# Softmax in PSUM, one subtraction for the rests of the turned probabilities, and global jobs in other slots

## The chip, the cores and the metric

The kernel runs on one core of a Trainium2 chip. The metric is the device time of one execution in microseconds (us). Five instruction streams of the core matter: TensorE (PE, matrix products, with its weight loads as PEld), VectorE (DVE), ScalarE (ACT), GpSimd (POOL) and SyncE (SP), which here only issues DMA transfers. SBUF is the working memory, PSUM the memory into which TensorE writes.

## The reference

Local and global attention over 8 batches and 8 heads, followed by a two-layer network. Per head there are 512 local and 32 global positions of 64 values each. A local query sees the 32 global keys and the local keys at most 32 positions away; a global query sees all 544 keys.

```python
s_g = scale * np.matmul(q_g, k_all.transpose(0, 1, 3, 2))
out_g = np.matmul(sm(s_g), v_all)
mask = np.abs(pos[:, None] - pos[None, :]) <= window
s_ll = np.where(mask, s_ll, -1000000000.0)
s_l = np.concatenate([s_lg, s_ll], axis=-1)
out_l = np.matmul(sm(s_l), np.concatenate([v_g, v_l], axis=2))
# x: the outputs of all heads side by side, 4352 tokens x 512
h = np.maximum(x @ w_in, 0.0)      # 512 -> 2048
return (h * h @ w_out)             # 2048 -> 512
```

`sm` is the softmax with 1e-9 added to the sum.

## The kernel before

**Slots.** The whole kernel is one loop over slots t = 0 to 145 (line 614). In slot t the local attention of head-half t (128 of them: 8 batches, 2 halves of 256 queries, 8 heads; 8 head-halves make one block of 256 tokens) is taken through scores and softmax, and finished in slot t + 1. Step m = t - 9 of the network runs in the same slot: 8 steps for each of 17 blocks, the last of which holds the global tokens. One step is 256 of the 2048 hidden columns: `gemm1` (tile h, two halves j), `act1` (relu and square, into pt), `act2` (gh) and, a slot later, `gemm2` (tile o, accumulated over the eight steps and brought out by `evac`).

**Split values.** From slot 16 on (`plain` is false) every product is made of rounded operands (float32r, "hi") and the rests that rounding left ("lo"): a b is hi hi + hi lo + lo hi. So every operand is rounded by a ScalarE copy (qk, v, ph, gh, x_h, gvh, pth) and gets its rest by a VectorE subtraction (second half of qk, v, the parts of ph/ml/pl, gl, x_l, gvl, ptl). The names in brackets are the tiles under which the profile shows them. Before slot 16 plain float32 products are used.

**One local head-half** from slot 16 on: `scores` (line 155; four products into one PSUM bank, tile s, with the small global score product gs beside it), `softmax1` (VectorE: add the mask, negate, and take the minimum, into the SBUF tile prob, twice 224 columns), `softmax2` (ScalarE: exponential in place in prob, with row sums into st), `softmax3` (VectorE: add 1e-9, reciprocal, two multiplications in place), `turn` (GpSimd copies the 16-bit halves of prob apart into planes in three copies, and a DMA transposes them into turned). In slot t + 1 `join` (GpSimd) puts the halves together in joined; `parts` (ScalarE) rounds them to ph; `parts_rest` (lines 243 to 248) makes three rests: into a quarter of ph, into ml (128 columns) and into pl (256 columns); `av` multiplies with v into the PSUM tile xa (nine products), and `x_evac` in slot t + 2 copies it to x_h and x_l.

**Global jobs.** A group of four heads of a batch is done in two pairs. Once its scores are collected in sg, a table (lines 694 to 709) lays its steps on slots and on places within a slot: `g_soft`, `g_exp`, `g_norm`, `g_turn`, `g_join` as for the local heads, `g_parts` (pth, ptl), `g_split_v` (gvh, gvl), `g_av` (13 products into tile gxo, which uses xa's bank, and a scaled copy to gxs) and `g_x` (four VectorE transposes of 32 x 32 into xg). There are 16 groups, so 32 pairs.

**Order.** Each engine's instructions keep the order in which the program text issues them (class `InOrder`, line 43) once the slot reaches 17; an instruction that waits holds up all behind it on its engine. Plain `nc.sync` transfers (gv, qr, weights, outputs) are placed by the scheduler. The pool p1 has one buffer for each tag, p2 two. raw (a head's input) has two buffers: the load of head t + 2 waits until head t's raw was last read, by the rest of v. The scores' bank s, the bank of xa and pt are single.

In slot t TensorE runs s, h (j = 0), h (j = 1), gs, o (j = 0), gxo if there is one, o (j = 1), xa. The loop's core around the change, before:

```python
if run: gemm1(m, 0)
split_v(t); softmax2(t); parts(t - 1)
softmax3(t); turn(t); load_head(t + 2)
# jobs at places 4 and 3, gemm1(m, 1), g_scores
split_qk(t + 1); act1(m)
parts_rest(t - 1); split_qk_rest(t + 1)
# gemm2(m - 1, 0), jobs at place 0, gemm2(m - 1, 1)
av(t - 1); act2(m)
```

## Time and profile before

| what | value |
|---|---|
| median of 3 runs | 1070.45 us (1070.18 to 1073.39) |
| profiled execution, own time | 1071.19 us |
| its span, first to last instruction | 1069.1 us |
| mean granted TensorE clock | 0.994 |
| busy TensorE / VectorE / ScalarE / GpSimd | 1029.5 / 867.7 / 721.5 / 385.0 us |
| slots 22 to 127 (first scores to first scores) | 798.55 us |

In rows of the profile the first name is the written tile and the names behind the arrow are read; nearly all lines carry L53, the helper that keeps the order, so groups are told apart by their tiles. A group's row ends with its busy time, the mean of one instruction in ns, and the idle time of its engine just before it with what ended that. In the timeline and in the chain of waits the first number is the start and the second the length, in us. In a table of stretches each engine's busy time is followed by its number of instructions, in the order PE, PEld, DVE, ACT, POOL, then the granted clock, the DMA share and GB/s. In a table of waits the numbers are the total in us, how often, and the longest.

### The profile page before, as it was taken

What the parts mean: (1) busy time and instruction counts of PE and PEld (TensorE: products, weight loads), DVE (VectorE), ACT (ScalarE), POOL (GpSimd) and SP (SyncE); (2) the same over time, 40 slices, a digit from 0 to 9 for tenths busy, and PEclk for the clock granted to TensorE, in tenths of its full rate; (3) what the DMA queues carried; (4) which work ended last, traced back from release to release, by engine and by line L of the source; (5) the groups of instructions that cost most, each with busy time, mean ns of one, the idle gap of its engine ahead of it and who ended that gap; (6) DMA issues with size and microseconds to landing.
All of it is one profiled execution on the core that took longest, in us unless ns stands there. A gap on an engine that the chain in (4) does not pass through costs nothing.

```text
span 1069.1 us, 20564 instructions
## 1 busy us (share of the span) xinstructions
PE 1029.5 (96%) x7040; PEld 902.3 (84%) x7040; DVE 867.7 (81%) x2445; ACT 721.5 (67%) x1743; POOL 385.0 (36%) x544
## 2 busy tenths in 40 slices
PE   8999989999999999999999999999999999999998
PEld 6776778988898888888888889888888888889896
DVE  5689878899989888898979999898989999893311
ACT  6889766767767766767666766776667676664432
POOL 1010344444445343444444443453445353441000
PEclk9999989999999999999999999999999999999999
DMA  9772444445444544454544444545444454341000
GB/s 367 310 258 80 104 103 115 114 116 125 116 123 101 136 103 101 115 118 123 122 115 116 116 120 109 123 104 125 125 110 105 118 135 110 103 95 54 5 21 20
DMA packets 193576, 127.69 MB, mean 119 GB/s; under 512 B 143552, under 2 KB 168640, under 8 KB 193472
## 3 DMA queue, kind: packets, MB, share of 16 engines
q1 hardware_dynamic: 193328, 126.32, 44.5%
q8 instruction: 55, 0.90, 0.4%
q14 instruction: 49, 0.40, 0.1%
q10 hardware_dynamic: 144, 0.07, 0.0%
HBM read 82.84 MB, written 8.91 MB: 86 GB/s over the span
## 4 chain that ended last, share of the span: by engine, by line
PE 43%; DVE 37%; ACT 8%; issue 5%; DMA 3%; POOL 2%; SPq 0%; DVEq 0%; POOLq 0%; ACTq 0%
PE o L53 17%; PE h L53 16%; DVE prob L53 6%; DVE st L53 5%; DVE qk L53 5%; PE xa L53 4%; ACT prob L53 3%; DVE v L53 3%; PE s L53 3%; DVE gl L53 2%; PE gxo L53 2%; DVE x_l L53 2%; DVE ph L53 2%; DVE pl L53 2%; DMA raw<-in_pk_dram 2%
## 5 line engine op out<-in xcount | busy, mean ns | idle before, releaser
L53 PE MATMUL h<-x_h,ws 128*128 128x256 f32 x2048 | 391.4, 284 | 0.0
L53 PEld LDWEIGHTS h<-x_h,ws 128*128 128x128 f32 x2048 | 329.1, 192 | 0.7
L53 PE MATMUL o<-ws,gh 128*128 128x512 f32 x1024 | 324.4, 398 | 3.2 <-ACT ot L53 3.0
L53 PE MATMUL h<-x_l,ws 128*128 128x256 f32 x1024 | 290.9, 284 | 1.1 <-DVE x_l L53 1.1
L53 POOL COPY joined<-turned 128x1024 uint16<-128x1024 uint16 x112 | 155.3, 1387 | 378.1 <-DMA turned<-planes 232.9
L53 POOL COPY planes<-prob 128x448 uint16<-128x448 uint16 x336 | 171.3, 547 | 152.1 <-DVE prob L53 152.1
L53 PEld LDWEIGHTS o<-ws,gh 128*128 128x128 f32 x1024 | 182.5, 189 | 38.2 <-ACT ot L53 7.0
L53 PE MATMUL o<-ws,gl 128*128 128x512 f32 x512 | 202.1, 395 | 0.0
L53 PEld LDWEIGHTS h<-x_l,ws 128*128 128x128 f32 x1024 | 197.0, 192 | 3.2 <-DVE x_l L53 2.6
L53 ACT ACTIVATE prob<-prob,st 128x224 f32<-128x224 f32 x224 | 106.3, 475 | 90.3 <-DVE st L53 89.5
L53 DVE TENSOR_TENSOR gl<-pt,gh 128x512 fp32r<-128x512 f32 x128 | 87.5, 684 | 73.2 <-ACT gh L53 72.0
L53 DVE TENSOR_TENSOR qk<-raw,qk 64x352 fp32r<-64x352 f32 x224 | 109.1, 487 | 8.7 <-ACT qk L53 1.6
L53 PEld LDWEIGHTS o<-ws,gl 128*128 128x128 f32 x512 | 96.3, 188 | 23.1
L53 ACT ACTIVATE pt<-h 128x512 f32<-128x512 f32 x128 | 74.2, 580 | 54.3 <-PE h L53 54.0
L53 ACT CAST x_h<-xa 64x256 fp32r<-64x256 f32 x120 | 43.7, 364 | 98.2 <-PE xa L53 97.9
L53 ACT CAST ph<-joined 128x512 fp32r<-128x512 f32 x112 | 68.9, 615 | 41.2 <-POOL joined L53 39.0
L53 PE MATMUL s<-qk 128*128 128x224 f32 x448 | 83.5, 298 | 8.2 <-DVE qk L53 5.6
L53 DVE TENSOR_SCALAR st<-st 128x2 f32<-128x2 f32 x128 | 62.5, 488 | 34.0 <-ACT prob L53 29.8
L53 ACT CAST qk<-raw 128x608 fp32r<-128x608 f32 x112 | 78.1, 697 | 8.7 <-DMA raw<-in_pk_dram 8.6
L53 DVE TENSOR_TENSOR v<-raw,v 128x192 fp32r<-128x192 f32 x112 | 80.5, 719 | 0.0
L53 DVE CUSTOM_DVE_ANT_0 prob<-s,con 128x224 f32<-128x224 f32 x224 | 77.7, 382 | 3.0 <-PE s L53 1.3
L53 ACT ACTIVATE pt<-pt 128x512 f32<-128x512 f32 x128 | 74.5, 582 | 4.0
(85 smaller groups left out, 1616.9 us busy)
## 6 DMA issues: line engine op xcount, KB each, us to landing
raw<-in_pk_dram SPq DMA_DIRECT2D x112, 400.0 KB, 3.5
wr<-in_w_dram SPq DMA_DIRECT2D x32, 512.0 KB, 8.0
gv<-in_vg_dram SPq DMA_DIRECT2D x32, 320.0 KB, 3.8
out_dram<-ot SPq DMA_DIRECT2D x32, 256.0 KB, 2.4
raw<-in_pk_dram SPq DMA_DIRECT2D x15, 432.0 KB, 8.2
qr<-in_qg_dram SPq DMA_DIRECT2D x31, 64.0 KB, 3.1
turned<-planes SPq DMA_TRANSPOSE x112, 3.1
out_dram<-ot SPq DMA_DIRECT2D x8, 64.0 KB, 1.7
```

Source lines behind the costliest of these rows:

```text
L53: r = method(*args, **kwargs)
```

## The change

It does the following.

- The softmax of the heads from 16 on works in the scores' bank: the masked minimum writes back into s, the exponential works in place there, and only the multiplication writes to prob. The row sums of the exponentials go to two columns behind xa (the tile is 258 columns wide now).
- `parts_rest` is one subtraction over 512 columns into pl; ml goes. `av` uses three slices of pl: the product with ml (128 columns) becomes one with 256 columns.
- The rest gl of a step is made in the next slot, behind `softmax1` (`act2_rest`).
- `split_qk` comes ahead of `parts`; the rests of qk, then of ph, then (from slot 22 on) of v follow `softmax3`.
- Both output tiles of a block are brought out together, ahead of `softmax1`, into buffers of gl and gh.
- `g_av` moves a slot on and into the scores' bank; the copy to gxs is a job of its own, with qr's buffer; `g_x` becomes a TensorE transpose into the 64 columns of s that the scores leave free, and two ScalarE copies to xg. `g_parts` moves for every other group, and the second pair's steps with it.

The diff, cut to its core:

```diff
...
 WCH = 32
+LATE = 22
...
     heads = {}
+    state = {"s": None}
...
     joined = cp.tile([P, 512], F32, name="joined")
-    ml = cp.tile([P, P], F32R, name="ml")
     nc.gpsimd.memset(planes, 0)
-    nc.gpsimd.memset(f(ml), 0.0)
     pt = ps_a.tile([P, 512], F32, name="pt")
...
         ac.copy(v[:, 0, :], raw[:, QK:])
+    def split_v_rest(t):
+        raw, v = heads[t]["raw"], heads[t]["v"]
         ve.tensor_sub(v[:, 1, :], raw[:, QK:], f(v[:, 0, :]))
...
         pool, tag = (ps_h, "h") if t < 8 and t % 2 else (ps_a, "s")
-        s = pool.tile([P, 2, WIN], F32, tag=tag, name=f"s{t}")
+        s = pool.tile([P, 512], F32, tag=tag, name=f"s{t}")
+        state["s"] = s
+        s = s[:, : 2 * WIN].rearrange("p (u n) -> p u n", u=2)
         for u in range(2):
...
         return 0.0625 if plain(t) else 0.125
+    def work(t, u):
+        hd = heads[t]
+        return hd["pr"][:, WIN * u : WIN * (u + 1)] if plain(t) else hd["s"][:, u, :]
...
             ve.tensor_tensor_reduce(
-                out=pr[:, WIN * u : WIN * (u + 1)],
+                out=work(t, u),
                 in0=hd["s"][:, u, :],
...
         st = heads[t]["st"]
-        pr = heads[t]["pr"]
+        su = st[:, 4:6] if plain(t) else state["xa"][:, HALF:]
         for u in range(2):
-            w_ = pr[:, WIN * u : WIN * (u + 1)]
+            w_ = work(t, u)
             ac.activation(
-                out=w_, in_=w_, func=AF.Exp, scale=-1.0, bias=st[:, u : u + 1], accum_out=st[:, 4 + u : 5 + u]
+                out=w_, in_=w_, func=AF.Exp, scale=-1.0, bias=st[:, u : u + 1], accum_out=su[:, u : u + 1]
             )
+        heads[t]["sums"] = su
     def softmax3(t):
-        st = heads[t]["st"]
-        pr = heads[t]["pr"]
-        ve.tensor_scalar(out=st[:, 6:8], in0=st[:, 4:6], scalar1=1e-9, scalar2=None, op0=ALU.add)
+        st, pr = heads[t]["st"], heads[t]["pr"]
+        ve.tensor_scalar(out=st[:, 6:8], in0=heads[t]["sums"], scalar1=1e-9, scalar2=None, op0=ALU.add)
         ve.reciprocal(out=st[:, 2:4], in_=st[:, 6:8])
         for u in range(2):
-            w_ = pr[:, WIN * u : WIN * (u + 1)]
+            to, by = pr[:, WIN * u : WIN * (u + 1)], st[:, 2 + u : 3 + u]
             if MUL <= t < NPLAIN:
-                ac.activation(out=w_, in_=w_, func=AF.Copy, scale=st[:, 2 + u : 3 + u])
+                ac.activation(out=to, in_=work(t, u), func=AF.Copy, scale=by)
             else:
-                ve.tensor_scalar(out=w_, in0=w_, scalar1=st[:, 2 + u : 3 + u], scalar2=None, op0=ALU.mult)
+                ve.tensor_scalar(out=to, in0=work(t, u), scalar1=by, scalar2=None, op0=ALU.mult)
...
-    def sides(z):
-        return z.rearrange("p (c n) -> p c n", n=128)[:, 0:4:3, :]
     def parts(t):
...
         ph = heads[t]["ph"]
-        pl = heads[t]["pl"] = p1.tile([P, 256], F32R, tag="pl", name=f"pl{t}")
-        ve.tensor_sub(ph[96:, 128:384], joined[64:96, 128:384], f(ph[64:96, 128:384]))
-        ve.tensor_sub(ml[:64, :], joined[:64, 192:320], f(ph[:64, 192:320]))
-        ve.tensor_sub(pl.rearrange("p (c n) -> p c n", c=2), sides(joined), sides(f(ph)))
+        pl = heads[t]["pl"] = p1.tile([P, 512], F32R, tag="pl", name=f"pl{t}")
+        ve.tensor_sub(pl, joined, f(ph))
+    def out_bank(t):
+        state["xa"] = ps_a.tile([P, HALF + 2], F32, tag="xa", name=f"xa{t}")
+        return state["xa"]
...
-            xa = ps_a.tile([P, HALF], F32, tag="xa", name=f"xa{t}")
+            xa = out_bank(t)[:, :HALF]
             v, pts = hd["raw"][:, c:], hd["pts"]
...
         else:
-            xa = ps_a.tile([64, HALF], F32, tag="xa", name=f"xa{t}")
+            xa = out_bank(t)[:64, :HALF]
             v, ph, pl = hd["v"], hd["ph"], hd["pl"]
...
                 o, vs, hs = xa[:, 128 * u : 128 * u + 128], slice(64 * u, 64 * u + 64), slice(384 * u, 384 * u + 128)
-                mm += [(o, v[:, 0, vs], ph[:, hs]), (o, v[:, 1, vs], ph[:, hs])]
-            mm += [(xa, v[:, i, 128:], ph[:, 128:384]) for i in range(2)]
-            mm.append((xa[:, 64:192], v[:, 0, 128:], ml))
-            for u in range(2):
-                o, vs, ps = xa[:, 128 * u : 128 * u + 128], slice(64 * u, 64 * u + 64), slice(128 * u, 128 * u + 128)
-                mm.append((o, v[:, 0, vs], pl[:, ps]))
+                mm += [(o, v[:, 0, vs], ph[:, hs]), (o, v[:, 1, vs], ph[:, hs]), (o, v[:, 0, vs], pl[:, hs])]
+            mm = [mm[0], mm[1], mm[3], mm[4], *((xa, v[:, i, 128:], ph[:, 128:384]) for i in range(2)), mm[2], mm[5]]
+            mm.append((xa, v[:, 0, 128:], pl[:, 128:384]))
         for i, (o, a, b) in enumerate(mm):
...
         heads[t] = None
-    state = {}
...
         (gvh, gvl), (pth, ptl) = state["gvs"], state["gpt"]
-        xo = ps_a.tile([64, P], F32, tag="xa", name=f"gxo{t}_{pair}")
+        xo = ps_a.tile([P, 512], F32, tag="s", name=f"gxo{t}_{pair}")[:64, :P]
         mm = []
...
             pe.matmul(xo, x, y, start=i == 0, stop=i == len(mm) - 1)
-        xs = p1.tile([64, P], F32, tag="xs", name=f"gxs{t}_{pair}")
+        state["xo"] = xo
+    def g_xs(t, pair):
+        xo = state["xo"]
+        xs = p1.tile([64, P], F32, tag="qr", name=f"gxs{t}_{pair}")
         ac.activation(out=xs, in_=xo, func=AF.Copy, scale=state["gst", t][:64, pair : pair + 1])
...
     def g_x(t, pair):
-        b, grp, xs = t // 16, (t // 4) % 2, state["xs"]
+        if state["s"] is None:
+            state["s"] = ps_a.tile([P, 512], F32, tag="s", name=f"xt{t}_{pair}")
+        xt = state["s"][:, 2 * WIN :]
+        pe.transpose(xt, state["xs"], ident[:64, :64])
+        state["xt"] = xt
+    def g_x_copy(t, pair):
+        b, grp, xt = t // 16, (t // 4) % 2, state["xt"]
         for j in range(2):
-            h = 4 * grp + 2 * pair + j
-            for dd in range(2):
-                r = (h % 2) * 64 + 32 * dd
-                ve.transpose(
-                    out=xg[r : r + 32, h // 2, 32 * b : 32 * b + 32],
-                    in_=xs[32 * j : 32 * j + 32, 64 * j + 32 * dd : 64 * j + 32 * dd + 32],
-                )
+            r = slice(64 * j, 64 * j + 64)
+            ac.copy(xg[r, 2 * grp + pair, 32 * b : 32 * b + 32], xt[r, 32 * j : 32 * j + 32])
...
         ac.copy(gh, r)
-        ve.tensor_sub(gl, r, f(gh))
         moe["g", m] = (gh, gl)
+    def act2_rest(m):
+        gh, gl = moe["g", m]
+        ve.tensor_sub(gl, moe["r"], f(gh))
...
         for i in tiles:
-            pool, tag = ((p1, "ptl"), (p1, "gvl"))[i]
+            pool, tag = ((p2, "gl"), (p2, "gh"))[i]
             ot = pool.tile([P, DM], F32, tag=tag, name=f"ot{blk}_{i}")
...
         if done:
-            evac(m // 8 - 1, (0,))
+            evac(m // 8 - 1)
         if live:
             softmax1(t)
+        if 8 < m <= NSTEP:
+            act2_rest(m - 1)
         if run:
...
             split_v(t)
+            if t < LATE:
+                split_v_rest(t)
+        for job, *args in jobs.pop((t, 7), ()):
+            job(*args)
         if live:
             softmax2(t)
-        if new:
-            parts(t - 1)
+        for job, *args in jobs.pop((t, 4), ()):
+            job(*args)
         if live and not early:
...
             turn(t)
+        for job, *args in jobs.pop((t, 9), ()):
+            job(*args)
+        if t + 1 < NT and not early:
+            split_qk(t + 1)
+        if new:
+            parts(t - 1)
+        if not early:
+            if t + 1 < NT:
+                split_qk_rest(t + 1)
+            if new:
+                parts_rest(t - 1)
+            if live and t >= LATE:
+                split_v_rest(t)
         if NPLAIN <= t + 2 < NT:
             load_head(t + 2)
-        for place in (4, 3):
-            for job, *args in jobs.pop((t, place), ()):
-                job(*args)
-        if done:
-            evac(m // 8 - 1, (1,))
+        for job, *args in jobs.pop((t, 3), ()):
+            job(*args)
         w_tick(t, 0)
+        if t >= NT:
+            state["s"] = None
         if live and early:
...
             scores(t + 1)
-        if t + 1 < NT and not early:
-            split_qk(t + 1)
         if run:
...
             split_qk(t + 1)
-        if new:
-            parts_rest(t - 1)
-        if t + 1 < NT:
             split_qk_rest(t + 1)
...
             d = t if t % 8 == 3 else t + 2
+            first = t % 8 == 3
+            k = d + 7 if first else d + 6
             for at, *job in (
...
                 (d + 4, 6, g_join),
-                (d + 4, 3, g_parts),
-                (d + 4, 0, g_av, 0),
-                (max(d + 5, 17), 3, g_x, 0),
-                (d + 5, 2, g_split_v, 1),
-                (max(d + 6, 17), 0, g_av, 1),
-                (max(d + 7, 18), 3, g_x, 1),
+                ((d + 5, 9, g_parts) if first else (d + 4, 3, g_parts)),
+                (d + 5, 0, g_av, 0),
+                (d + 5, 0, g_xs, 0),
+                (d + 6, 7, g_x, 0),
+                (d + 6, 4, g_x_copy, 0),
+                ((d + 6, 3, g_split_v, 1) if first else (d + 5, 1, g_split_v, 1)),
+                (k, 0, g_av, 1),
+                (k, 0, g_xs, 1),
+                (k + 1, 7, g_x, 1),
+                (k + 1, 4, g_x_copy, 1),
             ):
...
```

## The prediction

> **What bounds the kernel now.** First the page's totals and its chain of waits, then that chain in order of time, since a share over 1069 us mixes stages.
>
> ```profile
> span 1069.1 us, 20564 instructions
> PE 1029.5 (96%) x7040; PEld 902.3 (84%) x7040; DVE 867.7 (81%) x2445; ACT 721.5 (67%) x1743; POOL 385.0 (36%) x544
> PE 43%; DVE 37%; ACT 8%; issue 5%; DMA 3%; POOL 2%; SPq 0%; DVEq 0%; POOLq 0%; ACTq 0%
> ```
>
> TensorE looks full, yet 37% of the chain is VectorE's. The chain in order of time, where it never leaves TensorE:
>
> ```profile
> 519.70 0.49 PE s L53 x4
> 520.19 2.88 PE h L53 x24
> ...
> 526.00 0.65 PE xa L53 x9
> 526.65 0.49 PE s L53 x4
> ...
> 531.54 0.78 PE gxo L53 x13
> ...
> 534.41 0.49 PE s L53 x4
> ```
>
> One slot's own products last 526.65 - 519.70 = 6.95 us; with a global product (gxo) 534.41 - 526.65 = 7.76, so gxo adds 0.81. Now the steady stretch, slots 22 to 127, between their first scores: the engines' busy time, and two groups in it for the counts.
>
> ```profile
> 153.13:951.68 798.55, 776.64 (x5578) 692.16 (x5576) 717.90 (x2029) 559.73 (x1376) 348.03 (x484) 1.00 0.47 115
> L53 PE MATMUL s<-qk 128*128 128x224 f32 x420 | 76.8, 295 | 5.4 <-DVE qk L53 3.1
> L53 PE MATMUL gxo<-gvh,pth 128*64 128x128 f32 x125 | 24.8, 228 | 2.3 <-ACT pth L53 1.3
> ```
>
> 420 / 4 = 105 slots and 125 / 5 = 25 global products need 105 x 6.95 + 25 x 0.81 = 750.0 us; they took 798.55. **48.6 us are stalls**, and that is the sum that the change can reach. TensorE's waits in this stretch name their ends:
>
> ```profile
> PEld s L53 <- DVE qk L53: 13.0, 44, 0.4
> PEld gxo L53 <- DVE ptl L53: 10.4, 12, 0.9
> PEld o L53 <- ACT ot L53: 6.4, 8, 1.9
> ```
>
> They are shorter than the 48.6 because a wait also empties the pipeline of matmuls. The worst slot type (two of every sixteen, such as the one from 585.4 to 594.8, 9.39 us long) shows why VectorE is late:
>
> ```profile
> 588.55 1.62 DVE L53 TENSOR_SCALAR st<-st 128x2 f32<-128x2 f32 x1
> 590.94 1.04 DVE L53 TENSOR_TENSOR ptl<-sg,pth 128x512 fp32r<-128x512 f32 x1
> ```
>
> An addition over two columns (the softmax's sums) takes 1.62 us and ends with GpSimd's copy of the global probabilities; ptl, behind it, is what gxo waits for. In the ordinary slot shown below, with GpSimd still, the same addition takes 0.17.
>
> **The change, part by part: VectorE.** The groups of the whole run that it touches:
>
> ```profile
> L53 DVE TENSOR_TENSOR ph<-joined,ph 32x256 fp32r<-32x256 f32 x112 | 63.0, 563 | 9.2 <-ACT ph L53 5.8
> L53 DVE TENSOR_TENSOR ml<-joined,ph 64x128 fp32r<-64x128 f32 x112 | 34.2, 305 | 3.5
> L53 DVE TENSOR_TENSOR pl<-joined,ph 128x256 fp32r<-128x256 f32 x112 | 45.8, 409 | 0.0
> L53 DVE TENSOR_TENSOR gl<-pt,gh 128x512 fp32r<-128x512 f32 x128 | 87.5, 684 | 73.2 <-ACT gh L53 72.0
> L53 DVE TENSOR_SCALAR st<-st 128x2 f32<-128x2 f32 x128 | 62.5, 488 | 34.0 <-ACT prob L53 29.8
> L53 DVE TENSOR_TENSOR x_l<-xa,x_h 64x256 fp32r<-64x256 f32 x120 | 49.7, 415 | 21.7 <-ACT x_h L53 19.8
> L53 DVE STREAM_TRANSPOSE xg<-gxs 32x32 f32<-32x32 f32 x128 | 25.6, 200 | 1.3
> ```
>
> The three rests (0.56 + 0.31 + 0.41 = 1.28 us) become one over 512 columns: 0.68 like gl, 1.04 like the ptl above; 0.24 to 0.60 saved. The addition now reads its sums from PSUM; between the undisturbed 0.17 below and today's mean 0.49 I take 0.2, since x_l, which reads PSUM too, is steady at 0.415: 0.3 saved, 1.4 in the worst slots. Four 32x32 transposes per global product go: 0.8. The two multiplications now read PSUM: 0.38 rather than 0.36 each at most, like the masked minimum over the same 224 columns below. VectorE's 717.90 / 105 = 6.84 us per slot fall to about 5.9.
>
> **The order of a slot.** An ordinary slot beginning at 541.2, VectorE, ScalarE and the DMA queue:
>
> ```profile
> 542.56 0.39 DVE L53 CUSTOM_DVE_ANT_0 prob<-s,con 128x224 f32<-128x224 f32 x1
> 543.75 0.17 DVE L53 TENSOR_SCALAR st<-st 128x2 f32<-128x2 f32 x1
> 544.15 0.58 DVE L53 TENSOR_SCALAR prob<-prob,st 128x224 f32<-128x224 f32 x2
> 546.17 1.07 DVE L53 TENSOR_TENSOR qk<-raw,qk 64x352 fp32r<-64x352 f32 x2
> 544.13 0.70 ACT L53 CAST qk<-raw 128x608 fp32r<-128x608 f32 x1
> 546.44 0.59 ACT L53 CAST gh<-pt 128x512 fp32r<-128x512 f32 x1
> 546.43 1.24 SPq L53 DMA_TRANSPOSE turned<-planes  x1
> 547.76 0.53 SPq L53 DMA_DIRECT2D raw<-in_pk_dram  x1
> raw<-in_pk_dram SPq DMA_DIRECT2D x112, 400.0 KB, 3.5
> ```
>
> Changed, from the slot's start: gl of the slot before fills the hole between 1.75 (second masked minimum done) and 2.55 (today's addition), 0.68 long, so it costs nothing; without that hole the addition would be 0.7 late. Addition, reciprocal and multiplications end at 3.65. ScalarE's qk cast (now ahead of ph) starts at 2.9 as today, because raw, issued at 6.56, lands 3.5 later, at 10.06, which is 3.1 of the next slot; it ends at 3.8. The two qk rests follow until 4.9, pl until 5.6 (its ph, 512 columns like gh, 3.8 + 0.6 = 4.4), v's rest until 6.0. The next scores need the qk rests at 6.95 (today they end at 6.04, and 13.0 us of waits show how often later); the last xa products need pl at 6.8. Both have over a microsecond. So I cost these moves at nothing on TensorE. New waits, with what is queued behind: the scores' bank stays in use until the multiplications (3.65 of 6.95; behind: the next scores); in evacuation slots the output tiles take gh's and gl's second buffers, so the gh cast waits for the last o product (6.3) and ends at 6.9, with x_h of the next slot behind it, whose xa is done at 6.95. A global pair moves a slot on, so that its 13 products no longer meet ptl on the way; xs shares qr's buffer, so the small qr load waits for the transposing product and lands some 3 us after it, at about 5.2, when its cast is due at 5.3.
>
> **TensorE.** The product of 128 columns with ml becomes one of 256:
>
> ```profile
> L53 PE MATMUL xa<-ph,v 128*64 128x128 f32 x448 | 45.3, 223 | 0.4 <-ACT gxs L53 0.3
> L53 PE MATMUL xa<-ph,v 128*64 128x256 f32 x224 | 44.8, 281 | 2.2 <-DVE ph L53 2.2
> L53 PE MATMUL pt<-con,pr 128*128 128x128 f32 x32 | 6.5, 277 | 0.0
> ```
>
> 281 - 223 = 58 ns x 112 = **+6.5**. The 32 transposing products (64 columns) are new: between half of 6.5 / 32 = 0.20 us and the full 0.28 that one of 128 columns takes alone, so 32 x 0.10 to 0.28 = 3.3 to 9; taken **+5**, near the half, as the columns are half.
>
> **The start of the heads (slots 16 to 21, 56.3 us).** One stall there drags the clock:
>
> ```profile
> 139.00:142.50 3.50, 0.92 (x5) 0.52 (x5) 1.76 (x6) 1.26 (x3) 0.00 (x0) 0.88 0.97 226
> 142.50:149.00 6.50, 6.48 (x30) 6.31 (x31) 5.01 (x15) 4.65 (x12) 4.59 (x5) 0.54 0.26 91
> ```
>
> 2.6 us idle, then 6.5 at a granted 0.54. It is a raw load that was late (the qk cast waited for it), and VectorE is loaded with weight splits here. Removing it and its slow clock is worth 2.6 + 2.2 (24 h products at double their 0.12) plus some 2 of qk waits: 0 to 7, taken **-4**.
>
> **What stays of the 48.6.** One row of GpSimd:
>
> ```profile
> L53 POOL COPY sg<-gq 128x1280 uint16<-128x1280 uint16 x16 | 27.9, 1745 | 6.3 <-DMA gq<-gp 6.3
> ```
>
> The slots with g_join still hold this 1.75 us copy ahead of the planes copies; their planes end near 6.9 instead of the 5.2 at which the turning DMA is issued above, raw is issued at about 8.2 and lands 4.7 into the next slot, and the qk cast, with ph and relu behind it, shifts by 1.6. pl is then ready within 0.2 us of its need. I leave 0.6 for each of 13 global groups: **8** stay, with 0 and 48.6 as the ends.
>
> **Sum**, against the profiled execution: 1071.2 (span 1069.1 + 2.1 around it; the median of the runs is 0.7 lower) - 48.6 + 8 + 6.5 + 5 - 4 = **1038**. With everything at its good end 1071.2 - 48.6 + 6.5 + 3.3 - 7 = 1025.
>
> **Rivals.** (1) *ScalarE becomes the late one.* 559.73 / 105 = 5.33 us per slot leaves 1.6, but it is uneven: in an evacuation slot two output copies now stand ahead of the exponentials, the gh cast waits for the last o product, and a global exponential can follow it. If half of the stalls return in this form: 1071.2 - 24.3 + 11.5 - 2 = 1056. For it: ScalarE's order decides relu, gh and xs alike; against it: the 1.6 us and TensorE's two h buffers. The Trainium skill ("PSUM — Partial Sum Buffer", PSUM bank collisions raise a hardware error) says that two engines must not use the same quadrant of a bank at once; no row here shows it, but by it the first exponential, in place in the scores' bank, would have to wait for the second masked minimum, some 0.3 us, and for a transposing product. That would weigh for this rival.
>
> (2) *The raw loop, slower.* raw has two buffers, and v's rest, now last on VectorE, is what frees one. From raw's landing: qk cast, two rests, pl, v's rest, new load.
>
> ```profile
> L53 DVE TENSOR_TENSOR v<-raw,v x5: 355/976/1170, 604.4 to 634.1; 128x192 fp32r<-128x192 f32 x5
> ```
>
> At the low ends 0.70 + 0.98 + 0.68 + 0.36 + 3.5 = 6.2, under a slot; at the high ends, with v at 1.17, pl at 1.04, and the 1.24 us issue of the turning DMA in front, 0.70 + 1.07 + 1.04 + 1.17 + 1.24 + 3.5 = 8.7. It decides from 7.05 on, and loses from 7.6 = 798.55 / 105 on; at 8.1, between, 105 x 0.5 = 52 us: 1123. Against it: the planes copies, which make v and pl slow, are mostly over by 5.3, and the turning DMA's issue lies beside VectorE's work. [...]
>
> (3) *It doesn't do what it says*: the stalls are re-labelled, each later by one instruction, 1071 within 3.
>
> **Chances.** Forecast (1028 to 1047) 0.62; rival 1 (1048 to 1066) 0.20; rival 2 0.10; rival 3 0.05; below 1028 0.03. The range 1026 to 1060 leaves out rivals 2 and 3, the top of rival 1 and the bottom, some 0.19. A measurement here tells 0.3% (3 us) from no change: faster 0.85, same 0.05, slower 0.10.
>
> **What would show it.** Right: slots of 7.0 us (7.8 with gxo) following each other on TensorE in the chain; no wait of gxo on ptl and of o on ot; the st addition near 0.2 beside GpSimd copies; pl between 0.68 and 1.04; no stretch at a granted 0.54. Wrong: waits of s on qk that remain with the qk cast waiting for raw (rival 2), relu or gh ending later than 7 in their slots (rival 1), an addition that still shows 1 us, transposing products over 0.28 us. The forecast fails if slots average over 7.3.

## The result and the profile after

The changed kernel takes **1103.22 us** (median; 1100.98 to 1105.98) against 1070.32 for the kernel before on the same chip: a ratio of 1.0303, 95% interval 1.0272 to 1.0333. It is slower by 33 us, and the prediction (1038, range 1026 to 1060) was wrong by 65. The profiled execution took 1100.98. In the last run below, one execution of five took 3931 us at a granted TensorE clock of 0.246; the median given there is that of the other four.

The page of the changed kernel: span, busy time, and the chain of waits by engine and by line.

```profile
span 1099.2 us, 20364 instructions
PE 1035.5 (94%) x7072; PEld 903.9 (82%) x7072; DVE 771.1 (70%) x2093; ACT 729.9 (66%) x1807; POOL 403.6 (37%) x543
PE 42%; DVE 19%; DMA 15%; ACT 14%; POOL 4%; issue 4%; SPq 1%; DVEq 0%; ACTq 0%; POOLq 0%
PE o L54 16%; PE h L54 15%; DMA raw<-in_pk_dram 13%; PE xa L54 4%; DVE qk L54 4%; DVE s L54 4%; PE s L54 3%; ACT s L54 2%; DVE pl L54 2%; DMA turned<-planes 2%; POOL planes L54 2%; ACT qk L54 2%; ACT pt L54 2%; DVE x_l L54 2%; PE gxo L54 2%
```

VectorE did lose work: 771 us busy instead of 868, and 19% of the chain instead of 37%. But its share went to DMA (3% to 15%, nearly all of it raw) and to ScalarE (8% to 14%). The table of stretches, for slots 16 to 21 and 22 to 126, says where the time went:

```profile
94.44:156.85 62.41, 51.87 (x313) 41.06 (x310) 44.58 (x108) 38.85 (x95) 19.05 (x28) 0.95 0.31 80
156.85:979.48 822.63, 781.25 (x5617) 694.54 (x5615) 627.34 (x1718) 566.48 (x1430) 365.74 (x483) 0.99 0.47 112
```

The start of the heads takes 62.4 instead of 56.3, the steady stretch 822.6 instead of 798.6: +6.1 and +24.1, which is the 30.1 us by which the spans differ. The granted clock explains little of it: 0.992 in the mean of this execution, 0.994 before. VectorE is down to 5.97 us a slot (627.34 / 105), as forecast ("about 5.9"), and the slots are longer all the same.

A slot without global work (slot 73, the one that the prediction shows from 541.2), from TensorE's scores at 560.61 to the next at 567.55, on PE, VectorE, ScalarE and the DMA queue:

```profile
560.61 0.60 PE L54 MATMUL s<-qk 128*128 128x224 f32 x4
...
567.55 0.60 PE L54 MATMUL s<-qk 128*128 128x224 f32 x4
...
562.51 0.14 DVE L54 DVE_READ_ACCUMULATOR2_ANT st<- 128x1 f32 x1
...
564.20 0.81 DVE L54 TENSOR_SCALAR prob<-s,st 128x224 f32<-128x224 f32 x2
...
566.05 0.88 DVE L54 TENSOR_TENSOR pl<-joined,ph 128x512 fp32r<-128x512 f32 x1
...
562.68 0.42 ACT L54 ACTIVATE s<-s,st 128x224 f32<-128x224 f32 x1 [1.14 <-DVE st L54]
...
564.03 0.71 ACT L54 CAST qk<-raw 128x608 fp32r<-128x608 f32 x1 [0.33 <-DMA raw<-in_pk_dram]
...
566.42 1.23 SPq L54 DMA_TRANSPOSE turned<-planes  x1
567.82 0.46 SPq L54 DMA_DIRECT2D raw<-in_pk_dram  x1
```

The slot itself is 6.94 us, no longer than before, although the 256-column rest product is in it. But everything in it is later. Before, in the slot from 541.2, the second masked minimum ran from 542.56 to 542.95 (the prediction shows its row), and the first exponential beside it:

```profile
542.68 0.48 ACT L53 ACTIVATE prob<-prob,st 128x224 f32<-128x224 f32 x1 [0.54 <-DVE st L53]
```

That is 1.5 us into the slot; now it begins at 562.68, 2.07 into it, after the second minimum's result was read (562.51 + 0.14). The multiplications end at 564.20 + 0.81, that is 4.40 into the slot (3.65 forecast); the turning transposition is issued at 5.81, and raw behind it at 7.21 (6.56 forecast), already in the next slot. The qk cast starts at 3.42 and waits for raw (2.9 forecast), and pl ends at 6.32 (5.6 forecast), 0.3 before TensorE loads it. Here nothing is lost, but little slack is left.

Where a global group adds its work, that slack is gone. Three slots, from 596.76, 603.73 and 612.91, in a table of stretches; then GpSimd, the DMA queue, ScalarE and TensorE in order of time:

```profile
596.76:603.73 6.97, 6.97 (x53) 6.37 (x52) 5.89 (x19) 4.55 (x12) 4.69 (x7) 1.00 0.41 99
603.73:612.91 9.18, 7.37 (x53) 6.24 (x51) 6.83 (x16) 5.61 (x15) 5.88 (x7) 1.00 0.59 144
612.91:622.19 9.28, 9.28 (x65) 8.64 (x64) 6.97 (x20) 5.56 (x14) 2.98 (x4) 0.82 0.57 108
```

```profile
600.30 2.21 POOL L54 COPY gp<-sg 128x1088 uint16<-128x1088 uint16 x4
602.46 2.24 POOL L54 COPY planes<-prob 128x448 uint16<-128x448 uint16 x3
607.89 1.35 POOL L54 COPY joined<-turned 128x1024 uint16<-128x1024 uint16 x1 [3.20 <-DMA turned<-planes]
...
604.72 1.23 SPq L54 DMA_TRANSPOSE turned<-planes  x1
606.06 0.52 SPq L54 DMA_DIRECT2D raw<-in_pk_dram  x1
...
609.46 0.70 ACT L54 CAST qk<-raw 128x608 fp32r<-128x608 f32 x1 [2.10 <-DMA raw<-in_pk_dram]
...
610.73 0.69 PE L54 MATMUL xa<-ph,v 128*64 128x128 f32 x6 [0.61 <-ACT ph L54]
612.61 0.46 PE L54 MATMUL xa<-pl,v 128*64 128x128 f32 x3 [1.20 <-DVE pl L54]
```

GpSimd's four gp copies stand ahead of the planes copies, so the planes end at 604.70, a microsecond into the next slot; turned is issued at 604.72, raw at 606.06, and joined starts only when turned has landed, at 607.89. The qk cast waits 2.10 us for raw, ph stands behind it, and TensorE waits for ph and then for pl. The slot lasts 9.18, and the next one, which holds a gxo, 9.28 at a granted clock of 0.82.

This is only a part of what the change added. The same three slots took 24.10 us before (577.68 to 601.78), one gxo included, and take 25.43 now. Over slots 22 to 126, by their first scores, what goes beyond 6.95 us a slot and 0.81 a gxo sums up as follows: 27.4 us in the two places of sixteen in which a global group's probabilities are joined (22.4 before), 13.1 in the two places behind these, where a gxo stands now (0.2 before), 19.2 in the four places with a transposing product (5.5 before), and 12.1 in the others (20.5 before). That is 71.8 us in place of the 48.6.

These are the waits that the whole run now shows:

```profile
ACT s L54 <- DVE st L54: 85.5, 70, 2.8
ACT qk L54 <- DMA raw<-in_pk_dram: 83.6, 72, 3.9
PEld xa L54 <- DVE pl L54: 30.1, 37, 1.7
PEld xa L54 <- ACT ph L54: 21.1, 17, 2.8
```

The waits of o on ot are gone and those of gxo on ptl are down to 1.2 us, as forecast. Those of xa on pl and ph took their place, and gxo now waits 8.3 us for the multiplications, whose bank it shares.

### The profile page after: what moved, and what is told of

Its sections match the earlier page's. It is cut to its first block, busy times and chain, and to the rows that moved or that the text cites. A ratio compares the mean times of both kernels' runs of the same rounds, so it can differ in the third digit from the quotient of the medians.

```text
span 1099.2 us, 20364 instructions
## 1 busy us (share of the span) xinstructions
PE 1035.5 (94%) x7072; PEld 903.9 (82%) x7072; DVE 771.1 (70%) x2093; ACT 729.9 (66%) x1807; POOL 403.6 (37%) x543
## 4 chain that ended last, share of the span: by engine, by line
PE 42%; DVE 19%; DMA 15%; ACT 14%; POOL 4%; issue 4%; SPq 1%; DVEq 0%; ACTq 0%; POOLq 0%
PE o L54 16%; PE h L54 15%; DMA raw<-in_pk_dram 13%; PE xa L54 4%; DVE qk L54 4%; DVE s L54 4%; PE s L54 3%; ACT s L54 2%; DVE pl L54 2%; DMA turned<-planes 2%; POOL planes L54 2%; ACT qk L54 2%; ACT pt L54 2%; DVE x_l L54 2%; PE gxo L54 2%
## 5 line engine op out<-in xcount | busy, mean ns | idle before, releaser
L54 PE MATMUL h<-x_h,ws 128*128 128x256 f32 x2048 | 403.0, 287 | 0.0
L54 POOL COPY joined<-turned 128x1024 uint16<-128x1024 uint16 x112 | 152.3, 1360 | 383.7 <-DMA turned<-planes 317.0
L54 POOL COPY planes<-prob 128x448 uint16<-128x448 uint16 x336 | 190.2, 603 | 158.4 <-DVE prob L54 158.3
L54 ACT ACTIVATE s<-s,st 128x224 f32<-128x224 f32 x224 | 95.0, 424 | 136.5 <-DVE st L54 85.5
L54 DVE TENSOR_TENSOR qk<-raw,qk 64x352 fp32r<-64x352 f32 x224 | 125.7, 561 | 48.7 <-ACT qk L54 45.2
L54 ACT CAST qk<-raw 128x608 fp32r<-128x608 f32 x112 | 78.7, 703 | 84.4 <-DMA raw<-in_pk_dram 83.6
L54 DVE TENSOR_SCALAR prob<-s,st 128x224 f32<-128x224 f32 x224 | 90.7, 446 | 13.1 <-DVE st L54 0.5
L54 DVE TENSOR_TENSOR pl<-joined,ph 128x512 fp32r<-128x512 f32 x112 | 92.5, 826 | 5.9 <-ACT ph L54 5.9
L54 DVE CUSTOM_DVE_ANT_0 s<-s,con 128x224 f32<-128x224 f32 x224 | 88.4, 395 | 8.7 <-PE s L54 3.1
L54 DVE TENSOR_TENSOR x_l<-xa,x_h 64x256 fp32r<-64x256 f32 x120 | 49.8, 415 | 60.6 <-ACT x_h L54 59.4
L54 PE MATMUL xa<-ph,v 128*64 128x128 f32 (+1 forms) x672 | 72.7, 244 | 13.9 <-ACT ph L54 13.8
L54 PEld LDWEIGHTS xa<-ph,v 128*64 128x64 f32 x672 | 55.9, 135 | 34.9 <-ACT ph L54 21.1
```

Of the source, the lines that this page charges most:

```text
L54: r = method(*args, **kwargs)
```

## The experiments

Medians; the ratio is to the kernel before on the same chip. Three causes were tried on the changed kernel (raw late on the DMA queue; the softmax in the scores' bank; GpSimd's global copies ahead of the planes copies), then the single subtraction by itself.

### Why raw is late

The changed kernel with v's rest early in every slot (it is the last reader of raw):

```diff
-LATE = 22
+LATE = 200
```

> The changed kernel with v's rest in every slot where slots 16 to 21 have it (behind gl), so that raw is free some 4 us earlier. Theory A (raw's buffer is held by v's rest, now last on VectorE): ScalarE's wait for raw falls from 84 us to under 20, time 1060 to 1080. Theory B (raw is issued behind the turning transposition on SyncE's queue, and that is late because the softmax chain in the scores' bank and GpSimd's copies are late): raw is still issued right behind the transposition, the wait stays over 50 us, and the time stays within 10 us of 1103.

1105.39 us, ratio 1.033 (1.0309 to 1.0351), and the wait for raw is 102.7 us in all, no shorter than 83.6: theory B. Rival 2 of the prediction had v's rest hold the buffer; freed early, it gains nothing. So the load's place on the queue was moved:

```diff
-            raw = p2.tile([P, PS], F32, tag="raw", name=f"raw{t}")
+            raw = p2.tile([P, QK], F32, tag="raw", name=f"raw{t}")
...
+    def load_v(t):
+        rv = heads[t]["rv"] = p2.tile([P, PS - QK], F32, tag="rv", name=f"rv{t}")
+        sp.dma_start(rv, pk[t, :, QK:PS])
...
+        if NPLAIN <= t + 2 < NT:
+            load_head(t + 2)
         if live and not early:
             softmax3(t)
             turn(t)
...
-            load_head(t + 2)
+            load_v(t + 2)
```

> The changed kernel with a head's input loaded in two parts: the q and k columns (free since the slot before) ahead of the turning transposition, the v columns where the whole load stood. Both theories: ScalarE's wait for raw falls under 15 us. What it gains is what the late raw costs altogether: 30 to 50 us, so 1053 to 1073. If the time stays above 1090, raw is only the last of several late things (a third theory: the softmax chain itself, through the turned probabilities, sets the slot).

1091.68 us, ratio 1.0196 (1.0179 to 1.0213): **11.5 us** better than the changed kernel. The wait for raw, and the two stretches (slots 16 to 21, 22 to 126):

```profile
ACT qk L54 <- DMA raw<-in_pk_dram: 10.5, 8, 2.5
```

```profile
94.89:148.92 54.03, 49.04 (x312) 39.59 (x310) 44.86 (x109) 38.34 (x95) 20.65 (x28) 0.97 0.38 96
148.92:974.80 825.88, 784.33 (x5616) 700.21 (x5615) 657.57 (x1718) 564.76 (x1431) 377.83 (x484) 0.99 0.48 111
```

The wait falls from 83.6 to 10.5 us, but the time stays above 1090, where the expectation saw a third cause. In the profile most of the gain lies in the start (62.4 to 54.0) and none in the steady stretch. But this execution took 1095.8 us at a mean granted clock of 0.987, so a few us of gain in the steady stretch may not show in it. That raw was late there together with something else is the likelier reading, not a shown one.

### The scores' bank

The changed kernel with the probabilities in SBUF again, and only the row sums left in PSUM:

```diff
     def work(t, u):
         hd = heads[t]
-        return hd["pr"][:, WIN * u : WIN * (u + 1)] if plain(t) else hd["s"][:, u, :]
+        return hd["pr"][:, WIN * u : WIN * (u + 1)]
```

> The changed kernel with the probabilities in SBUF (tile prob) as before, and only the row sums in PSUM. Theory B: the first exponential no longer waits for the second masked minimum, planes, transposition and raw each start 0.7 to 0.9 us earlier, the wait for raw falls to under 40 us, time 1065 to 1085. Theory A: v's rest ends as late as before against raw's landing, the wait for raw stays over 60 us, time 1095 to 1105.

1079.65 us, ratio 1.0093 (1.0063 to 1.0122): **23.6 us** better. The time is theory B's, but its mechanism is not: the wait for raw is 88.1 us, where B had under 40. So the bank did not make that wait longer. The same edit from the other end, the kernel before with its softmax in the bank (sums in SBUF as before):

```diff
-                out=pr[:, WIN * u : WIN * (u + 1)],
+                out=pr[:, WIN * u : WIN * (u + 1)] if plain(t) else hd["s"][:, u, :],
...
-            w_ = pr[:, WIN * u : WIN * (u + 1)]
+            w_ = pr[:, WIN * u : WIN * (u + 1)] if plain(t) else heads[t]["s"][:, u, :]
...
```

> The kernel before with one part of the change alone: the masked minimum and the exponential of the heads from 16 on work in place in the scores' bank; the row sums stay where they were, in SBUF, and so the addition on them stays as it was, beside GpSimd's copies. Theory A, the engines take turns in the bank: the first exponential starts some 0.5 us later than before, behind the second masked minimum, and the two multiplications take 0.45 instead of 0.36 us each; before's order has some slack, so 1075 to 1095. Theory B, the place of the softmax costs nothing by itself: within 3 of 1070.

1114.56 us, ratio 1.0413 (1.0391 to 1.0435): 45 us slower, well above both theories. The bank alone costs more than the whole change does.

The transposing product of the global outputs shares that bank. The changed kernel with VectorE's four transposes back in its place:

```diff
...
-        xt = state["s"][:, 2 * WIN :]
-        pe.transpose(xt, state["xs"], ident[:64, :64])
+        for j in range(2):
+            h = 4 * grp + 2 * pair + j
+            for dd in range(2):
+                r = (h % 2) * 64 + 32 * dd
+                ve.transpose(
+                    out=xg[r : r + 32, h // 2, 32 * b : 32 * b + 32],
+                    in_=xs[32 * j : 32 * j + 32, 64 * j + 32 * dd : 64 * j + 32 * dd + 32],
+                )
...
-                (d + 6, 7, g_x, 0),
+                (d + 6, 3, g_x, 0),
...
```

> The changed kernel with the global outputs turned by four VectorE transposes of 32 x 32, as before, instead of one TensorE product and two ScalarE copies. If the transposing product costs 0.5 us in each of its 32 slots, as the starts of the products beside it in slots 1, 7 and 8 of sixteen say: 14 to 18 us less, 1085 to 1090, whatever holds raw. If its cost is only the 0.1 to 0.28 us of the product itself: 3 to 9 us less, or nothing where the VectorE transposes (0.8 us) take it back.

1159.42 us, ratio 1.0834 (1.0814 to 1.0854), slower than any expectation, and inconclusive on the product. xs shares qr's buffer and is now read later in the slot, so qr comes late (its cast waits 68.9 us for it in all) and the global jobs with it, and the next scores wait for gxs:

```profile
PE s L54 <- ACT gxs L54: 31.5, 7, 5.1
```

### GpSimd's order

First the two edits that helped, together:

> The changed kernel with two edits together: the columns of q and k are loaded ahead of the turning transposition, and the probabilities stay in SBUF, with only the row sums in PSUM. Apart the two gained 11.5 and 23.6 us. Theory A, they are two causes: 1103.2 - 11.5 - 23.6 = 1068 within 4. Theory B, they are one chain, so that the gains overlap: 1074 to 1080.

1068.45 us, ratio 0.9984 (0.9971 to 0.9996). 1103.2 - 11.5 - 23.6 = 1068.1: they add, and the kernel is back where the one before was, no better. On top of it, GpSimd's work for the global heads behind the planes copies (place 9 is behind `turn`, place 6 at the slot's start):

```diff
-                (d + 3, 6, g_turn),
-                (d + 4, 6, g_join),
-                ((d + 5, 9, g_parts) if first else (d + 4, 3, g_parts)),
+                (d + 3, 9, g_turn),
+                (d + 4, 9, g_join),
+                (d + 5, 9, g_parts),
```

> The kernel with both edits (q and k loaded ahead, probabilities in SBUF) and one more: GpSimd's work on the global probabilities (copying apart, putting together) stands behind the local heads' planes copies in its order instead of ahead of them, and the rounding of the global probabilities comes a slot later for half of the groups. Theory A, what is left is GpSimd's global copies ahead of the planes copies, which make the turned probabilities late in two slots of every sixteen: 1040 to 1055. Theory B, those copies are hidden or only move the lateness to the join of the next slot: within 4 of the kernel without this edit.

1036.33 us, ratio 0.9682 (0.9658 to 0.9706), faster than either theory. In this version the second group's global probabilities are rounded only after the next batch's global scores have begun to overwrite them, so its global outputs are not those of the reference and its time alone is of use. The next version rounds them in time, with the second group's jobs a slot earlier:

```diff
-            d = t if t % 8 == 3 else t + 2
+            d = t if t % 8 == 3 else t + 1
...
-                (d, 2, g_load_v, 0),
+                (d if first else d + 1, 2, g_load_v, 0),
```

> The kernel with q and k loaded ahead and the probabilities in SBUF, and GpSimd's global work behind the local heads' planes copies. In the run before this one, the second group's global probabilities were rounded only after the next batch's global scores had begun to be written over them, so that part was not the reference's; here the second group's jobs start a slot earlier and are rounded in time. Theory A, the order of GpSimd's copies was what was left: 1036 within 4. Theory B, that run was fast because the second group's rounding came late and off the busy slots: 1044 to 1060.

**1035.82 us, ratio 0.9681 (0.9658 to 0.9703)**: the fastest version, 34 us below the kernel before and 67 below the changed one. Its steady stretch, and GpSimd and the DMA queue in the two slots that answer to the pair above (558.9 to 565.9 and 565.9 to 572.8):

```profile
146.63:917.16 770.53, 764.43 (x5604) 692.21 (x5602) 636.49 (x1715) 569.08 (x1426) 383.75 (x483) 1.00 0.51 119
```

```profile
562.89 1.68 POOL L54 COPY planes<-prob 128x448 uint16<-128x448 uint16 x3 [0.26 <-DVE prob L54]
564.51 2.80 POOL L54 COPY gp<-sg 128x1088 uint16<-128x1088 uint16 x4
567.78 1.37 POOL L54 COPY joined<-turned 128x1024 uint16<-128x1024 uint16 x1 [0.47 <-DVE x_l L54]
...
564.60 1.24 SPq L54 DMA_TRANSPOSE turned<-planes  x1
```

turned is issued at 564.60, within its slot, and joined waits no longer for it. Against the 750 us that the prediction worked out as the floor, 20.5 us are left. gp's copies themselves became slower (2.80 instead of 2.21): it is their place that counts.

With only g_turn moved:

> The kernel with q and k loaded ahead and the probabilities in SBUF (1068), and only the copies that take the global probabilities apart (gp) moved behind the planes copies; the copy that puts them together (sg from gq) stays ahead of them. Theory A, gp's copies were the late ones, since the long stalls lie in the slots behind them (2.25 and 1.56 us of each sixteen slots): 1041 to 1047. Theory B, the 1.75 us copy into sg, which the prediction named, is as much to blame: 1050 to 1060.

1048.97 us, ratio 0.9801 (0.9776 to 0.9825), between the two theories: of the 32.6 us, the place of gp's copies is worth 19.5. The other 13 are for the rest of the edit together: the copy into sg behind the planes copies, and g_parts and the second group's jobs at other places.

### Are the causes separate?

The changed kernel with the new GpSimd order alone (both edits above):

> The changed kernel with GpSimd's new order alone (softmax in the scores' bank, raw loaded behind the turning transposition as in the change). Theory A, three causes that add up: 1103 - 32 = 1071 within 5. Theory B, with raw and the bank still late GpSimd's order buys less, since planes are late anyway: 1080 to 1098.

1109.9 us, ratio 1.0379 (1.0347 to 1.0411): neither theory; the same edit now costs 7 us. The DMA queue and ScalarE around the slot that begins at 520.6:

```profile
522.15 1.32 SPq L54 DMA_TRANSPOSE gq<-gp  x1
523.57 0.53 SPq L54 DMA_DIRECT2D raw<-in_pk_dram  x1
...
527.42 0.70 ACT L54 CAST qk<-raw 128x608 fp32r<-128x608 f32 x1 [2.38 <-DMA raw<-in_pk_dram]
```

The transposition into gq, which waits for gp, now stands ahead of raw on the queue, and raw is issued 2.9 us into the slot: an edit of GpSimd's order moved a DMA past another. So q and k have to be loaded ahead first. With that, and the softmax still in the bank:

> The changed kernel with q and k loaded ahead and GpSimd's new order, but the softmax left in the scores' bank. Theory A, GpSimd's new order needs q and k loaded ahead (alone it puts the global transposition ahead of raw on the DMA queue), and with that the bank's 24 us are a cost of their own: 1059 within 4. Theory B, the bank was only late because the rest was, and its price shrinks: 1038 to 1050.

1075.77 us, ratio 1.0049 (1.0033 to 1.0066): neither theory. GpSimd's order now gains 16 us (from 1091.7) where alone it lost 7, and the bank costs 40 (1075.8 against 1035.8), not 24 and not less. Its price seems to depend on what stands behind the multiplications, as three rows of waits suggest: of the changed kernel, of this one, and of the kernel before with its softmax in the bank:

```profile
POOL planes L54 <- DVE prob L54: 158.3, 74, 42.4
```

```profile
POOL planes L54 <- DVE prob L54: 168.2, 95, 42.4
```

```profile
POOL planes L53 <- DVE prob L53: 194.4, 103, 44.7
```

The planes copies wait for prob 74 times where the bank costs 24 us (67 times in the changed kernel with q and k loaded ahead, where it costs 23: 1091.7 against 1068.5), and 95 and 103 times where it costs 40 and 45. Where GpSimd's global copies hold the planes, later multiplications hide behind them; elsewhere each passes its lateness on to turned, joined and ph. That is argued from the counts; no run set it apart.

### The single subtraction

The kernel before with one subtraction for the three rests and the 256-column product, xs in qr's buffer:

```diff
-        ve.tensor_sub(ph[96:, 128:384], joined[64:96, 128:384], f(ph[64:96, 128:384]))
-        ve.tensor_sub(ml[:64, :], joined[:64, 192:320], f(ph[:64, 192:320]))
-        ve.tensor_sub(pl.rearrange("p (c n) -> p c n", c=2), sides(joined), sides(f(ph)))
+        ve.tensor_sub(pl, joined, f(ph))
...
-            mm.append((xa[:, 64:192], v[:, 0, 128:], ml))
+            mm.append((xa, v[:, 0, 128:], pl[:, 128:384]))
...
```

> The kernel before with one part of the change alone: the three rests of the turned probabilities become one subtraction over 512 columns into pl, and the product with ml (128 columns) becomes one with 256. (The small buffer xs shares qr's buffer here, for want of room.) Theory A, the subtraction was a wrong step: beside GpSimd's copies it takes 1.04 us and loses what it saves, so 1070 within 4. Theory B, the part is good and the loss lies elsewhere: VectorE saves 0.4 to 0.6 us per slot where it is late (the waits of s on qk, 13 us, and of gxo on ptl, 10 us, shrink), and the 256-column product costs TensorE 0 to 6.5 us: 1052 to 1066.

1084.04 us, ratio 1.0128 (1.0104 to 1.0152), slower than either theory allows. To tell the shared buffer from the rest:

```diff
-        st = p2.tile([P, 8], F32, tag="st", name=f"st{t}")
+        st = p1.tile([P, 8], F32, tag="st", name=f"st{t}")
...
-        xs = p1.tile([64, P], F32, tag="qr", name=f"gxs{t}_{pair}")
+        xs = p1.tile([64, P], F32, tag="xs", name=f"gxs{t}_{pair}")
```

> The kernel before with the single subtraction and the 256-column product alone, and now with a buffer of its own for xs (the room comes from the statistics of the softmax, which get one buffer instead of two). Theory A, the loss of 13 us in the first trial came from xs waiting for qr: 1052 to 1066. Theory B, it came from shorter slots that move VectorE's multiplications and subtractions into GpSimd's global copies: 1075 to 1086.

1087.84 us, ratio 1.0173 (1.0136 to 1.021): the time is above theory B too, so the shared buffer was not it, unless st's single buffer costs as much. The multiplications as a group, in the kernel before and then in this one, and one slot of this one on VectorE and GpSimd:

```profile
L53 DVE TENSOR_SCALAR prob<-prob,st 128x224 f32<-128x224 f32 x224 | 70.6, 357 | 3.9
```

```profile
L53 DVE TENSOR_SCALAR prob<-prob,st 128x224 f32<-128x224 f32 x224 | 101.7, 496 | 3.9
```

```profile
473.64 3.08 DVE L53 TENSOR_SCALAR prob<-prob,st 128x224 f32<-128x224 f32 x2
...
473.64 1.35 POOL L53 COPY joined<-turned 128x1024 uint16<-128x1024 uint16 x1 [3.27 <-DVE st L53]
474.90 1.69 POOL L53 COPY sg<-gq 128x1280 uint16<-128x1280 uint16 x1
```

The two multiplications, 0.6 us by themselves, last 3.08 and end when GpSimd's copy into sg does (476.7 and 476.6); only then can the planes copies start. In the kernel before it was the addition that met this copy (its 1.62 us in the prediction). Here joined comes later in the slot, and both multiplications meet two copies; that it is later because the slots ahead of it became shorter is argued, not shown. Part of the loss may be the clock: its mean is 0.980 in this execution (1094.93 us) and 0.994 before, and if TensorE had been the limit throughout, that would be some 15 us, an estimate from 1093 x 0.020 - 1069 x 0.006. Last, the fastest version with the three subtractions and ml put back (the edit above, reversed):

> The kernel with all three edits, but with the rests of the turned probabilities as before the change: three subtractions, and the product of 128 columns with ml. Theory A, VectorE has slack once nothing else is late, so one subtraction or three is the same: within 4 of the kernel with all three edits. Theory B, VectorE's 0.6 us per slot more comes back as waits for the rests: 8 to 30 us slower than it.

1060.95 us (median of four), ratio 0.991 (0.9884 to 0.9937), 25 us slower than with one subtraction: theory B. The same edit loses 14 us in the kernel before (17 with the other buffers) and gains 25 once the rest is in order.

## Why the prediction was wrong, point by point

**What bounds the kernel** held: some 48 us of stalls above a floor of 6.95 us a slot, and a kernel with nearly the same parts that leaves 20 of them. The fastest version runs its steady stretch in 770.5 us, where the terms of the sum give 798.55 - 48.6 + 8 + 6.5 + 5 = 769.5. That agreement is one of the total and partly luck, since single terms were off, as told below. What failed is the claim that this change gets there.

**VectorE**: mostly right. The groups of the changed kernel:

```profile
L54 DVE TENSOR_TENSOR pl<-joined,ph 128x512 fp32r<-128x512 f32 x112 | 92.5, 826 | 5.9 <-ACT ph L54 5.9
L54 DVE TENSOR_SCALAR prob<-s,st 128x224 f32<-128x224 f32 x224 | 90.7, 446 | 13.1 <-DVE st L54 0.5
L54 DVE TENSOR_SCALAR st<-xa 128x2 f32<-128x2 f32 x112 | 17.8, 159 | 69.8 <-ACT s L54 69.8
```

pl takes 0.83 (0.68 to 1.04 forecast) and the addition 0.16 wherever it falls (0.2). Only the multiplications were mis-sized, 0.446 against 0.38 at most; the masked minimum was no good model for them.

**The order of a slot** is the step that failed: "So I cost these moves at nothing on TensorE." Its two margins of over a microsecond rested on multiplications that end at 3.65 and on raw issued at 6.56. The multiplications end at 4.40, because the first exponential must wait for the second minimum and because they take 0.81 themselves, and raw comes at 7.21. The runs price it: 24 us for the bank and 11.5 for raw on the changed kernel, together a little more than the 33 by which the kernel is slower.

The mechanism of the first stood in rival 1. The Trainium skill ("PSUM — Partial Sum Buffer", PSUM bank collisions raise a hardware error) says that two engines must be kept apart on one bank and quadrant. The trace agrees: the exponential starts 0.03 us after the minimum's result, where before the two overlapped. I priced the rival by half of the old stalls, 24 us, and named ScalarE's slots as the place. The four pairs of kernels give 23 to 45 us for the bank alone, and its place is ahead of the planes, turned and joined.

**Rival 3**, stalls that are only re-labelled, would have left the time at 1071; the stalls grew. **Rival 2** named the right wait, the qk cast on raw, and the wrong holder. v's rest is not to blame (first experiment); the load stands behind the turning transposition on the DMA queue, and that is late.

**The start** was forecast at -4 and came at +6.1. A stretch at half the granted clock is still there (145.5 to 152.3). With q and k loaded ahead the start takes 54.0, and 52.0 in the fastest version, which is 4.3 below the kernel before: the size was right, once raw is on time. One of its terms was not: 24 h products of 0.12 us, doubled, cost 2.9 and not 2.2.

**"What stays of the 48.6"**, taken as 8, is the other failure. With the bank and raw put right (the run of the two edits together), slots 22 to 126 still take 802.3 us (145.42 to 947.73), 52 above the floor; the new order of GpSimd's global copies brings them to 770.5. The term looked at the copy into sg only; gp's copies count for more (19.5 us, against 13 for the rest of that edit). They also got slower, from 29.4 to 35.8 us in all, by the short ones. The group rows of these, before and after the change:

```profile
L53 POOL COPY gp<-sg 128x64 uint16<-128x64 uint16 x48 | 10.2, 249 | 0.0
```

```profile
L54 POOL COPY gp<-sg 128x64 uint16<-128x64 uint16 x48 | 17.9, 409 | 0.0
```

Beside them now run, for most of the short copies' time, qk's rests and pl, all with two SBUF inputs; before, it was mostly multiplications and additions. By the Trainium skill ("SBUF — State Buffer", Who interferes with whom) such an instruction contends with a GpSimd instruction that reads SBUF. That agrees with the longer copies; the prediction lengthened pl and v for the copies beside them, and not the copies. By the Trainium skill ("SBUF — State Buffer", Who interferes with whom), too, a VectorE instruction in a 2-port mode, which a multiplication like these can enter, and GpSimd exclude each other: whichever issues first holds the other off for its whole instruction. That fits the multiplications of 3.08 us above and the old addition of 1.62, though no run shows the mode itself.

**TensorE**: +6.5 for the 256-column product did not show. It is 284 ns long in the first row below, but the slot quoted above with it in is still 6.94. The transposing product is 0.27 long, at the top of its range (0.10 to 0.28), and waits for the second minimum besides. Two slots of the fastest version, one with such a product and one without, follow the two rows:

```profile
L54 PE MATMUL xa<-pl,v 128*64 128x256 f32 x112 | 31.8, 284 | 0.0
L54 PE MATMUL s<-con,gxs 64*128 64x64 f32 x28 | 7.6, 272 | 8.4 <-DVE st L54 7.8
```

```profile
627.63:634.96 7.33, 7.33 (x53) 6.55 (x52) 5.70 (x16) 5.76 (x15) 3.05 (x4) 1.00 0.37 89
634.96:641.92 6.96, 6.96 (x52) 6.35 (x51) 4.88 (x14) 4.50 (x11) 3.05 (x4) 1.00 0.41 99
```

So the product costs its slot 0.37 us where nothing is late, some 12 us for 32 of them by that estimate, against the +5 of the sum. In the changed kernel the slots with one lose 19 us in the steady stretch, other waits included. No run took the product out by itself.

## What to carry to other kernels

Follow a late operation to the end of its chain before calling a move free: here multiplications that ended 0.75 us later than reckoned made the planes, the transposition, the join and the next load late, and the load shares its queue with the transposition. A saving is worth what the order lets through: the same subtraction cost 14 us in one order and gained 25 in another. And put work that nobody needs soon (the global copies) behind work that the next slot waits for, on every queue that it touches.

## What the runs showed of the hardware

Two VectorE multiplications from SBUF to SBUF beside GpSimd's copies took 3.08 us instead of 0.58, ending with the copy. Over all profiles kept here, one such multiplication takes 0.33 to 0.34 us while no GpSimd copy runs and up to 1.73 when one runs at its start. The same operation reading PSUM takes 0.44 to 0.45 either way, and the addition from PSUM 0.14 to 0.16. TensorE's waits of 0.61 and 1.20 us at the end of one slot were followed by a granted clock of 0.50 for 3.4 us (613.10 to 616.51) in the next.
